# 137 GpSimd operations of an attention-and-FFN kernel each get a wait on the VectorE operation planned just ahead of them

## The chip, the cores and the metric

The kernel runs on one core of a Trainium2 chip. The metric is the device time of one execution in microseconds (us), from the runtime's own measurement; a run's time is a little longer than the span that the hardware profiler sees between the first and the last instruction. Names in the profile: PE is TensorE's matmul, PEld its weight load, DVE is VectorE, ACT is ScalarE, POOL is GpSimd, SP is SyncE, which only issues DMAs here.

## The reference, cut to what matters

Two stages follow each other. The first is causal attention with a choice of key chunks: for every query only the 6 chunks of 32 keys with the largest upper bound take part. The second is a gated feed-forward layer on the result.

```python
# q, k, v: (4, 8, 768, 64) float32
ub = np.sum(np.maximum(q*k_min, q*k_max), axis=-1)        # per query and chunk of 32 keys
top_chunks = np.argsort(np.where(causal, ub, -1e9))[..., -6:]
scores = q @ k.T / 8, kept where chunk is chosen and key <= query
attn = exp(scores - max) / sum;   x = (attn @ v) as (3072, 512)
gate = sigmoid(x @ w_gate);       out = (gate * (x @ w_val)) @ w_out      # d_ff 1536
```

## The kernel before, in words

**Tiling.** The 3072 tokens are cut into eight units, u0 to u7, of up to 384 tokens (three blocks of 128). For a unit the kernel chooses chunks (`choose`, lines 868 to 915: bounds on PE into `ub`, then on VectorE `ubn` transposes, `mx` finds the eight largest, `ap` compares with the sixth, `apt` transposes back, and `hqm` copies the result into the masked rows of `hqe`/`hqo`), attends (`attend`, lines 918 to 978: `sc` scores on PE, `exp` on ScalarE, `cm` the causal mask on GpSimd at line 952, `pv` on PE; then `rz` and `x` on VectorE, lines 987 and 989), and runs the feed-forward layer (`ffn`: `g` and `v` products on PE, `tanh` on ScalarE, `hg` on VectorE at line 1258, `o` on PE). Units 5 to 7 form part of the gate product, and units 4 to 7 the output product, from seven block products instead of eight. These need sums of blocks: `tw` (line 1031) and `ss` (1136) of weights, `sw`/`sx` (1047) of activations, `tt` (1149) of x. Units overlap in time: while one is in its feed-forward layer the next attends.

**What sets the order.** Every operation is recorded with `plan.add` under a name such as `cm_u4_6` (causal mask, unit 4, head 6), with the engines that may run it and the buffers it reads and writes. Nothing is decided at run time: the string `ORDER` names all operations in the order in which they are emitted, each with its engine (P, A, V, G, S for PE, ScalarE, VectorE, GpSimd, SyncE), and `SLOTS` gives each buffer its place. Both strings are the outcome of an earlier planning. Each engine runs its own operations strictly in that order. Between engines only semaphores order the work; they come from the data: an instruction waits for the writers of what it reads and for the readers of what it overwrites. An engine that has nothing to wait for starts its next operation at once, whatever time the plan had for it.

**GpSimd's work** is one list of 256 operations: masks (`cm`, `cmf`), casts of v into `v16` (line 651), copies and casts through the helper at line 434 (`hk`, `hq`, `hqm`, `k16`, `kn`, `qn`, `held`), sums (`tw`, `ss`, `sw`, `tt`, lines 1031, 1047, 1136, 1149), and, early on, the issue of the ten DMAs that load the feed-forward weights (`wg`, `wv`, `wo`). Many of these copies and sums can be on VectorE as well, and the plan has put some there. In `plan.add`, `port=True` marks operations for the planning as users of what GpSimd and VectorE have in common on the way to SBUF. It has no effect on what is emitted.

The loop that emits all this is the last statement of the kernel's function:

```python
    for op in plan.order():
        op.emit(op.engine)
```

Of the kernel before, what the change touches and what calls it, by code (L numbers as in the profile page):

```python
# [115 lines left out]
hk1_u1_0=G v16_0_2=G wo2=G mx1_u1=V ap1_u1=V apt1_u1=V hqm1_u1_0=V g_u0_5=P tanh_u0_5=A v_u0_5=P exp_u1_1_1=A hqm1_u1_2=A g_u0_6=P  # L116
# [7 lines left out]
kn_u2_0=G kT_u2_0=P kt_u2_0=A v_u0_11=P rz_u1_2=V xT_u1_0=V x_u1_2=V xps_u1_2=P q3_u2=S qn_u2_3=G qT_u2_3=P cm_u1_7=G pv_u1_7=P  # L124
# [5 lines left out]
hk1_u2_1=G hk0_u2_0=V hk0_u2_3=G kt_u2_2=A g_u1_1=P tanh_u1_1=A hk0_u2_2=A g_u1_0=P tanh_u1_0=A o0_u0_2=P expf_3_1=A cmf_3_0=G  # L130
# [3 lines left out]
hqm0_u2_2=G hq0_u2_3=G v16_0_4=G exp_u2_5_0=A cm_u2_5=G exp_u2_5_1=A exp_u2_0_0=A cm_u2_0=G v16_0_5=G hq1_u2_2=G hqm1_u2_2=G  # L134
# [18 lines left out]
x_u3_2=V qf0_u4_1=V sc_u3_1_1=P g_u2_2=P hqm1_u3_2=G sc_u3_6_2=P exp_u3_2_1=A sc_u3_0_1=P exp_u3_6_2=A tanh_u2_2=A sc_u3_6_0=P  # L153
exp_u3_6_0=A sc_u3_6_1=P exp_u3_6_1=A exp_u3_0_1=A g_u2_1=P tanh_u2_1=A sc_u3_1_2=P exp_u3_1_2=A sc_u3_1_0=P exp_u3_1_0=A
exp_u3_1_1=A hk0_1_3=G cm_u3_2=G pv_u3_2=P k01_2=S k11_2=S k10_2=S k00_2=S v_2_0=S k16_2_2=G kx1_2_1=V kx1_2_3=V kx0_2_1=V
k16_2_0=V out_u1_1=S o0_u1_2=P sc_u3_3_0=P exp_u3_3_0=A cm_u3_0=G pv_u3_0=P sc_u3_3_1=P exp_u3_3_1=A o1_u1_2=P sc_u3_3_2=P
# [17 lines left out]
qf0_u6_2=V hk0_2_3=G cm_u4_2=G v16_2_3=G k16_3_2=G k16_3_1=G osb_u2_1=V out_u2_1=S k16_3_0=V kt_3_2=V qm_u5_2=G sc_u4_0_1=P  # L174
# [5 lines left out]
hg_u3_7=V pv_u4_3=P sc_u5_0_0=P v_3_1=S q10_3=S q11_3=S q00_3=S q01_3=S xT_u4_0=S sc_u4_6_3=P exp_u4_6_3=A sc_u4_5_2=P  # L180
exp_u4_5_2=A sc_u4_6_2=P sc_u4_6_0=P exp_u4_6_0=A exp_u4_6_2=A sc_u4_6_1=P exp_u4_6_1=A cm_u4_4=G pv_u4_4=P cm_u4_5=G pv_u4_5=P
hq0_u5_2=G v16_2_2=G g_u3_10=P tanh_u3_10=A mx1_u5=V rz_u4_1=V ap1_u5=V x_u4_1=V kx0_3_2=V rz_u4_2=V apt1_u5=V x_u4_2=V kx1_3_2=V
xT_u4_2=S exp_u5_0_0=A sc_u5_1_0=P exp_u5_1_0=A sc_u5_1_2=P sc_u5_1_1=P sc_u5_0_2=P v16_2_4=G hqm0_u5_2=G g_u3_8=P tanh_u3_8=A
cm_u4_6=G pv_u4_6=P rz_u4_3=V hk0_3_1=G cm_u5_0=G exp_u5_1_2=A exp_u5_1_1=A v_u3_8=P hg_u3_8=V x_u4_3=V kt_3_0=V cm_u5_1=G
k16_3_3=G hqm1_u5_0=G v_3_3=S v_3_4=S xT_u4_1=S out_u2_2=S qf1_u6_2=V exp_u5_0_2=A sc_u5_2_0=P exp_u5_2_0=A sc_u5_2_2=P
sc_u5_3_1=P exp_u5_3_1=A sc_u5_3_2=P exp_u5_3_2=A sc_u5_3_0=P exp_u5_3_0=A pv_u5_1=P pv_u5_0=P v_u3_10=P hg_u3_10=V rz_u5_0=V
qf1_u6_3=V kt_3_3=V hq1_u5_2=G v16_3_0=G hqm1_u5_2=G sc_u5_4_1=P exp_u5_2_2=A exp_u5_4_1=A sc_u5_2_1=P sc_u5_5_0=P exp_u5_5_0=A
# [14 lines left out]
hg_u4_2=V tw0_1=G sc_u5_7_2=P hq1_u7_2=G exp_u5_7_0=A exp_u5_7_1=A exp_u5_7_2=A pv_u6_4=P pv_u6_5=P rz_u6_2=V x_u6_2=V apt1_u7=V  # L202
# [10 lines left out]
sw0_u4_1=V pv_u6_7=P sw1_u4_1=V rz_u6_3=V rz_u5_3=V sc_u7_4_0=P exp_u7_4_0=A xT_u6_1=S xT_u6_2=S sc_u7_4_3=P sc_u7_1_3=P  # L213
exp_u7_1_3=A sc_u7_4_1=P sc_u7_1_0=P exp_u7_1_0=A cm_u7_1=G exp_u7_4_3=A sc_u7_1_1=P exp_u7_4_1=A exp_u7_1_1=A p1_u4=P p1z_u4=P
p1s_u4=V ss1_g4=G sw1_u4_2=G sw3_u4_2=G sc_u7_1_2=P exp_u7_1_2=A x_u5_3=V pv_u7_2=P pv_u7_7=P x_u6_3=V tw2_2=V sc_u7_5_2=P
exp_u7_5_2=A p2_u4=P sc_u7_6_2=P exp_u7_6_2=A sc_u7_5_1=P sc_u7_6_0=P exp_u7_6_0=A exp_u7_5_1=A p2z_u4=P p6_u4=P p6z_u4=P c11_u4=V
sw3_u4_1=G sc_u7_6_3=P exp_u7_6_3=A sc_u7_5_3=P exp_u7_5_3=A sc_u7_5_0=P pv_u7_1=P sc_u7_6_1=P exp_u7_6_1=A sc_u7_4_2=P p5_u4=P
# [7 lines left out]
c3_g2_u5=V c12_g2_u5=V p7_g4_u5=P p4_g4_u5=P pv_u7_3=P rz_u7_1=V p1_g3_u5=P m1_g3_u5=A ss3_g4=G p5_g4_u5=P p3_g4_u5=P held_u4_5=G  # L225
c22_g2_u5=V x_u7_1=V c21_g2_u5=V tt0_u6=G p2_g3_u5=P p6_g3_u5=P p7_g3_u5=P p4_g3_u5=P cm_u7_5=G ss3_g3=G pv_u7_5=P pv_u7_4=P
# [22 lines left out]
hg_u6_7=V held_u6_2=G sw2_u6_0=G sw2_u6_2=G sw1_u6_0=G sw2_u6_1=G v_u6_6=P p1s_u6=A tanh_u6_6=A tanh_u7_3=A hg_u6_6=V sw0_u6_1=G  # L249
# [11 lines left out]
u4_u7=V p7_u7=P p7z_u7=P c12_u7=V c22_u7=V c21_u7=V out_u7_1=S out_u7_0=S held_u6_5=A p2z_u67=P p6_u67=P p6z_u67=P p5_u67=P  # L261
# [89 lines left out]
p1_u7:5 p26_u7:6 p5_u7:2 p3_u7:7 p7_u7:1 p4_u7:3 p1_u67:7 p26_u67:0 p5_u67:4 p3_u67:5 p7_u67:6 p4_u67:2  # L351
"""


def act(n, psum=True, parts=128):
    took = (170 if psum else 195) + n / 1.2
    return (took - 105 if parts == 128 else took + 10, took)
# [22 lines left out]
def kernel(  # L380
# [10 lines left out]
    nc = tc.nc  # L391
# [44 lines left out]
    def lone(name, shape, dtype=F16):  # L436
        return keep.tile(shape, dtype, tag=name, name=name)

    ident32 = lone("ident32", [128, 128], F32)
    ident16 = lone("ident16", [128, 128])  # L440
# [12 lines left out]
    def const(name, engines, emit, reads=(), writes=(), prio=-2.0, port=False):  # L453
        plan.add(name, engines, emit, reads, writes, prio, port=port)
# [93 lines left out]
    for i in range(2):  # L548
        const(f"kcr{i}", {DVE: (270, 280)}, lambda e, i=i: nc.vector.memset(kcr[i], 0.0),
              writes=[("kcr", i, jb, p, m) for jb in range(NBLK) for p in range(NP) for m in range(2)], prio=-8 if i == 0 else -1)  # L550
    for e_ in range(2):
        const(f"hq{e_}", {DVE: (150, 160)}, lambda e, e_=e_: nc.vector.memset(hq[1][e_][MASK[e_], :, 0:64], 0.0),
              writes=[("hqm", 1, e_, p, "zero") for p in range(NP)])
    for i in range(2):
        const(f"ap{i}", {DVE: (400, 410)}, lambda e, i=i: nc.vector.memset(ap[i], 0.0),
              writes=[("ap", i, 0), ("ap", i, 1)], prio=-0.5 + i)
        const(f"v1{i}", {POOL: (260, 300)}, lambda e, i=i: nc.gpsimd.memset(v16[i][:, :, :, D:D + 1], 1.0),
              writes=[("v16", i, jb) for jb in range(NBLK)], prio=-9 + 6 * i)
        for e_ in range(2):
            for o in range(2):  # L560
# [3 lines left out]
                      reads=[epat], writes=[("hkp", i, e_, p) for p in range(o, NP, 2)], prio=0.3 + 0.2 * i, port=True)  # L564
# [8 lines left out]
    for i in range(30):  # L573
        keep_awake(i)
    const("ident16", {DVE: (150, 230)}, lambda e: nc.vector.tensor_copy(ident16, ident32),
          reads=["ident32"], writes=["ident16"], prio=-1.0)


    wgs = moe_w_gate.rearrange("(c p) f -> p c f", p=128)
# [535 lines left out]
    for n, w in enumerate(combos):  # L1115
        if n < 6:
            b = Buf("v", f"ss_{w[0]}{w[1]}", [128, 4, 2, 128], F16)
# [272 lines left out]
    attend(units[7], 7.0)  # L1390
    ffn(units[7], 8.0, 0.95)

    for op in plan.order():
        op.emit(op.engine)


# [28 lines left out]
```

## Time and profile before

| | us |
|---|---|
| three runs, median (lowest to highest) | 282.64 (281.72 to 282.82) |
| the profiled execution | 283.43 |
| its span in the profile | 281.7 |
| VectorE busy, share of the span | 235.7, 84% |
| ScalarE busy | 180.5, 64% |
| GpSimd busy | 163.3, 58% |

The profiled execution is 1.7 us longer than its span, and 0.8 us longer than the median of the three runs. Its TensorE clock was granted in full (9 in all 40 slices of the page). "Busy" is the time in which an engine had an instruction in work; in the timeline a row gives an instruction's start, its length, and in brackets the time that its engine sat idle before it with what ended the wait. Rows of equal instructions that follow each other are merged (x3).

### The profile page before, as it was taken

How to read it: one execution, taken by the hardware profiler on the slowest of the kernel's cores; microseconds unless marked ns; L12 is line 12 of the kernel's file. 1: busy time of each engine (PE TensorE's matmuls, PEld its weight loads, DVE VectorE, ACT ScalarE, POOL GpSimd, SP SyncE). 2: the span in 40 equal slices, each digit the busy share in tenths (PEclk: the TensorE clock that was granted, in tenths of full speed). 3: DMA queues.
4: the chain of work that ended last, by engine and by line, in shares of the span. 5: the costliest groups of instructions: out<-in, count | busy, mean ns of one | idle time of the engine just before them, and what ended most of it. 6: DMA issues, size and time to landing. Idle time of an engine off the chain costs nothing.

```text
span 281.7 us, 7507 instructions
## 1 busy us (share of the span) xinstructions
PE 268.8 (95%) x2806; PEld 188.9 (67%) x2806; DVE 235.7 (84%) x686; ACT 180.5 (64%) x386; POOL 163.3 (58%) x262
## 2 busy tenths in 40 slices
PE   5868989999999999999999999999999999999994
PEld 4645657667855665556687657776888688778683
DVE  4889846697998998886999987977889998888885
ACT  6377868669957943559689979987983422341520
POOL 5797743638464781823869956842685568063450
PEclk9999999999999999999999999999999999999999
DMA  6999999899999598977897230100310033000304
GB/s 161 246 254 204 205 216 209 180 192 210 178 214 182 131 195 162 199 142 141 164 154 111 63 89 16 40 0 2 73 74 2 1 81 126 2 1 2 150 2 150
DMA packets 131717, 34.70 MB, mean 123 GB/s; under 512 B 119776, under 2 KB 128736, under 8 KB 131680
## 3 DMA queue, kind: packets, MB, share of 16 engines
q1 hardware_dynamic: 126912, 29.50, 50.2%
q0 software_dynamic: 4768, 4.72, 10.0%
q8 instruction: 22, 0.36, 0.6%
q14 instruction: 15, 0.12, 0.1%
HBM read 30.67 MB, written 6.29 MB: 131 GB/s over the span
## 4 chain that ended last, share of the span: by engine, by line
PE 81%; DMA 9%; DVE 6%; issue 1%; SPq 1%; POOL 0%; DVEq 0%; POOLq 0%
PE v_u L1237 19%; PE g_u L1237 14%; PE o_u L1286 11%; PE sc_u L935 11%; PE p_u L1060 10%; PE pv_u L968 6%; DMA wg<-in_moe_w_gate_dram 6%; PE p_g_u L1169 5%; PE ube_u L874 3%; DMA kq_u<-in_k_dram 2%; DMA kf<-in_k_dram 1%; DVE x_u L989 1%; DVE tw L1031 1%; DVE ox L1077 1%; DVE hg_u L1258 1%
## 5 line engine op out<-in xcount | busy, mean ns | idle before, releaser
L946 ACT ACTIVATE att_u<-sc_u 128x512 f16<-128x512 f32 (+3 forms) x184 | 86.8, 571 | 8.6 <-PE sc_u L935 7.3
L1237 PE MATMUL v_u<-xT_u,wv 128*128 128x384 f16 x384 | 72.4, 326 | 0.1
L1258 DVE SCALAR_TENSOR_TENSOR hg_u<-gate_u,v_u 128x384 f16<-128x384 f16 x96 | 51.0, 544 | 18.6 <-ACT gate_u L1249 9.3
L1249 ACT ACTIVATE gate_u<-g_u 128x384 f16<-128x384 f32 x72 | 35.2, 498 | 42.2 <-PE g_u L1237 36.9
L1237 PE MATMUL g_u<-xT_u,wg 128*128 128x384 f16 x288 | 56.0, 326 | 2.1 <-DMA wg<-in_moe_w_gate_dram 1.5
L952 POOL TENSOR_SCALAR_AFFINE_SELECT att_u<-att_u 128x384 f16<-128x384 f16 (+1 forms) x56 | 28.5, 517 | 40.9 <-ACT att_u L946 39.8
L1237 PEld LDWEIGHTS <-wv 128*128 128x128 f16 x384 | 36.1, 98 | 20.5 <-DMA wv<-in_moe_w_val_dram 0.4
L1237 PEld LDWEIGHTS <-wg 128*128 128x128 f16 x288 | 26.7, 98 | 19.5 <-DMA wg<-in_moe_w_gate_dram 3.0
L1286 PE MATMUL o_u<-wo,hg_u 128*128 128x512 f16 x144 | 34.3, 379 | 0.0
L968 PE MATMUL pv_u<-v,att_u 128*128 128x65 f16 x640 | 26.3, 193 | 0.0
L968 PEld LDWEIGHTS <-att_u 128*128 128x128 f16 x640 | 24.2, 98 | 2.9 <-issue 0.6
L1206 DVE TENSOR_TENSOR f_g_u<-p_g_u,f_g_u 128x192 f32<-128x192 f32 (+1 forms) x72 | 24.9, 384 | 1.0 <-PE p_g_u L1169 0.4
L935 PE MATMUL sc_u<-hqe,hke 128*128 128x128 f16 (+2 forms) x220 | 25.4, 243 | 0.2
L935 PE MATMUL sc_u<-hqo,hko 128*128 128x128 f16 (+2 forms) x220 | 24.1, 243 | 0.1
L1286 PEld LDWEIGHTS <-hg_u 128*128 128x128 f16 x144 | 13.7, 98 | 13.4
L935 PEld LDWEIGHTS <-hke 128*128 128x128 f16 x220 | 16.5, 98 | 5.3 <-issue 0.8
L935 PEld LDWEIGHTS <-hko 128*128 128x128 f16 x220 | 16.4, 98 | 4.7 <-issue 0.4
L651 POOL CAST v<-v 128x512 f16<-128x512 f32 x23 | 14.5, 633 | 3.0 <-DMA v<-in_v_dram 2.5
L1249 ACT ACTIVATE gate_u<-f_g_u 128x384 f16<-128x384 f32 x24 | 11.9, 519 | 5.6 <-DVE hg_u L1258 2.9
L989 DVE TENSOR_TENSOR x_u<-pv_u,rz_u 128x384 f16<-128x384 f32 (+1 forms) x28 | 14.6, 524 | 0.9 <-DMA xT_u<-x_u 0.5
L897 DVE MAX8 mx_u<-ubn_u 128x8 f32<-128x8 f32 (+16 forms) x152 | 12.7, 159 | 0.3
L841 DVE STREAM_TRANSPOSE qf_u<-q 128x384 f32<-128x384 f32 (+2 forms) x28 | 11.7, 437 | 1.2 <-DMA q<-in_q_dram 1.2
(187 smaller groups left out, 507.9 us busy)
## 6 DMA issues: line engine op xcount, KB each, us to landing
v<-in_v_dram SPq DMA_DIRECT2D x23, 256.0 KB, 4.7
k<-in_k_dram SPq DMA_DIRECT2D x12, 384.0 KB, 5.5
q<-in_q_dram SPq DMA_DIRECT2D x12, 384.0 KB, 5.5
out_dram<-osb_u SPq DMA_DIRECT2D x12, 256.0 KB, 3.4
out_dram<-sw SPq DMA_DIRECT2D x8, 256.0 KB, 2.1
wv<-in_moe_w_val_dram POOLq DMA_DIRECT2D x3, 512.0 KB, 10.2
wo<-in_moe_w_out_dram POOLq DMA_DIRECT2D x3, 512.0 KB, 18.9
qf<-in_q_dram SPq DMA_DIRECT2D x8, 128.0 KB, 3.4
```

Of the source, the lines that this page charges most:

```text
L651: plan.add(f"v16_{b}_{ib}", {POOL: pool(H * D)}, lambda e: nc.gpsimd.tensor_copy(v16[b % 2][:, ib, :, 0:D], at(t)), reads=[t], writes=[("v ...
L935: nc.tensor.matmul(at(t)[:, o:o + 128 * m], hk[b % 2][e_][:, p, 128 * jb:128 * jb + 128], hq[u.side][e_][:, p, 128 * x:128 * (x + m)], sta ...
L946: plan.add(f"exp_{u.name}_{h}_{y}", {ACT: act(n)}, lambda e, t=t, att=att, b0=b0, n=n: nc.scalar.activation(at(att)[:, b0:b0 + n], at(t), ...
L952: nc.gpsimd.affine_select(out=dv, in_=dv, compare_op=ALU.is_ge, fill=0.0, base=0, pattern=[[0, u.m], [1, 128]], channel_multiplier=-1)
L968: nc.tensor.matmul(at(pv)[:, last, x, :], at(att)[:, c:c + 128], v16[b % 2][:, jb, h, :], start=(jb == 0), stop=(jb == ib))
L989: plan.add(f"x_{u.name}_{p}", {DVE: dve(u.t)}, lambda e: nc.vector.tensor_tensor(at(x_).rearrange("p a (e d) -> p e a d", e=2), at(pv)[:, ...
L1060: nc.tensor.matmul(at(to)[:, side], a(j)[:, i], b(j)[:, i], start=j == i == 0, stop=j == 2 and i == 1)
L1206: plan.add(f"{p}_{name}", {POOL: pool2(192 * n), DVE: dve(192 * n)} if slow else {DVE: dve(192 * n)}, lambda e: both(e).tensor_tensor(dst( ...
L1237: nc.tensor.matmul(at(t), w16[:, c, 128 * fb:128 * fb + 128], at(u.xt)[:, c, :], start=(c == 0), stop=(c == 3))
L1249: plan.add(f"tanh_{u.name}_{fb}", {ACT: act(T, not seven[0])}, lambda e, gv=gv, gate=gate: nc.scalar.activation(at(gate), gv(), AF.Tanh, s ...
L1258: plan.add(f"hg_{u.name}_{fb}", {DVE: dve(T)}, lambda e, vv=vv, gate=gate, hg=hg, fb=fb: nc.vector.scalar_tensor_tensor(at(hg)[:, fb % 2], ...
L1286: nc.tensor.matmul(at(o), at(hgs[fc // 2])[:, fc % 2, 128 * tb:128 * tb + 128], wo16[:, fc, lo:hi], start=(fc == 0), stop=(fc == NFB - 1))
```

## The change

A string `TIES` lists 137 pairs `a<b`: `a` is an operation of GpSimd and `b` the operation of VectorE that the plan has ending last before `a` starts. As each `a` is emitted, it is given a dependency on the last instruction of `b`, with a semaphore, as if `a` read what `b` wrote. Nothing else of the program moves: the order on every engine, the engines, the buffers and the data are the same. In the built program GpSimd waits for VectorE's semaphore in 163 places instead of 47; its instructions that do nothing but wait are 120 instead of 60, since a wait beyond an instruction's own goes into one of these ahead of it. ScalarE and TensorE lose one such wait each, which the new ones imply. `ident16` is marked `port=True`, which emits nothing.

```diff
+TIES = """
+hqm0_u1_2<hqm0_u1_0 v16_0_3<hg_u0_1 hk1_u1_0<ubm1_u1 v16_0_2<hg_u0_2 v16_0_1<hqm1_u1_0 cm_u1_1<hk1_u1_3 qn_u2_2<kcr1
...
+hq0_u4_2<qm_u4_2 hq0_u4_0<qf0_u6_1 hq1_u4_0<qf0_u6_3 kcr_2<hg_u2_11 hk0_2_2<mx1_u4 cm_u4_1<qf0_u5_2 cm_u4_2<hg_u3_0
+k16_3_2<qf0_u6_2 qm_u5_2<k16_3_0 cm_u4_7<kt_3_1 cm_u4_3<hqm0_u5_0 cm_u4_5<rz_u4_0 hq0_u5_2<hg_u3_6 v16_2_2<hg_u3_7 v16_2_4<rz_u4_1
+hqm0_u5_2<x_u4_1 cm_u4_6<kx0_3_2 hk0_3_1<rz_u4_2 cm_u5_0<x_u4_2 k16_3_3<rz_u4_3 hqm1_u5_0<x_u4_3 v16_3_0<qf1_u6_2
+hqm1_u5_2<rz_u5_0 cm_u5_3<qf1_u6_3 hk1_3_1<kt_3_3 hq0_u7_2<hk0_3_3 cm_u5_5<qf0_u7_1 v16_3_2<x_u5_1 hq0_u7_0<ubn1_u6
+hqm1_u6_2<hqm1_u6_0 v16_2_5<rz_u5_2 cm_u6_3<x_u5_2 cm_u6_2<ubn1_u7 cm_u6_4<mx1_u7 hqm0_u6_0<rz_u6_1 cm_u6_5<x_u6_1 tw0_1<hg_u4_0
+hq1_u7_2<hg_u4_2 cm_u6_0<tw0_0 cm_u6_1<ap0_u7 cm_u5_7<apt0_u7 v16_3_5<hqm0_u7_2 cm_u7_7<tw1_1 v16_3_3<ss0_g4 sw2_u4_0<tw2_1
+cm_u7_2<hg_u4_6 cm_u6_7<hg_u4_7 cm_u7_1<sw0_u4_1 ss1_g4<rz_u5_3 sw1_u4_2<p1s_u4 sw3_u4_1<x_u6_3 cm_u7_6<tw2_2 cm_u7_3<tw3_1
...
+sw2_u6_2<c4_g3_u7 sw1_u6_0<c12_g3_u7 sw2_u6_1<hg_u6_7 sw1_u67_0<sw0_u7_0 sw3_u7_0<hg_u7_4 sw1_u7_1<hg_u7_11 sw3_u7_2<sw1_u67_2
+sw3_u67_2<c11_u7 sw3_u67_1<u4_u7 sw2_u67_2<c12_u7
+"""
...
-          reads=["ident32"], writes=["ident16"], prio=-1.0)
+          reads=["ident32"], writes=["ident16"], prio=-1.0, port=True)
...
+    ties = {}
+    for w in TIES.split():
+        a, b = w.split("<")
+        ties.setdefault(a, []).append(b)
+    ends = {}
+    traced = nc.cur_bb.bb.instructions
     for op in plan.order():
+        n = len(traced)
         op.emit(op.engine)
+        for b in ties.get(op.name, ()):
+            tc.add_manual_dep(traced[n], ends[b], mybir.DependencyInfo(mybir.DependencyClass.Sync, mybir.DependencyReason.DATA), reason="tie")
+        ends[op.name] = traced[-1].name
```

More of the change, by code (lines that the diff above doesn't have):

```diff
@@ L352 @@
 """
+TIES = """
+hqm0_u1_2<hqm0_u1_0 v16_0_3<hg_u0_1 hk1_u1_0<ubm1_u1 v16_0_2<hg_u0_2 v16_0_1<hqm1_u1_0 cm_u1_1<hk1_u1_3 qn_u2_2<kcr1
+cm_u1_5<rz_u1_0 cm_u1_4<x_u1_0 kn_u2_0<qf_u2_2 qn_u2_3<rz_u1_2 cm_u1_7<xT_u1_0 cm_u1_6<x_u1_2 qm_u2_1<hg_u0_11 hq1_u2_1<kx1_u2_0
+hq0_u2_1<rz_u1_3 vc_3<qm_u2_3 hk1_u2_1<kcr_u2 hk0_u2_3<hk0_u2_0 cmf_3_1<hqm1_u2_0 cm_u2_4<hqm0_u2_0 hqm0_u2_2<rzf_3_1
+hq0_u2_3<xf_3_1 cm_u2_1<hg_u1_2 k16_1_1<kx0_1_3 hk1_u2_2<rz_u2_0 cm_u2_3<hg_u1_1 cm_u2_2<rz_u2_2 cm_u2_6<rz_u2_1 cm_u2_7<x_u2_1
+k16_1_3<x_u2_3 cm_u3_5<hqm0_u3_0 cm_u3_4<qf0_u4_0 cm_u3_2<qf0_u4_3 k16_2_2<x_u3_2 cm_u3_0<qf0_u4_1 hk1_1_3<kx1_2_1 v16_1_5<kx1_2_3
+cm_u3_3<k16_2_0 cm_u3_7<kt_2_2 hk1_2_0<rz_u3_0 k16_2_3<kx0_2_0 v16_2_0<hg_u2_0 k16_2_1<rz_u3_3 hk0_2_0<x_u3_1 v16_2_1<qf1_u4_0
+hq0_u4_2<qm_u4_2 hq0_u4_0<qf0_u6_1 hq1_u4_0<qf0_u6_3 kcr_2<hg_u2_11 hk0_2_2<mx1_u4 cm_u4_1<qf0_u5_2 cm_u4_2<hg_u3_0
[5 more added lines that the diff above has]
+cm_u7_2<hg_u4_6 cm_u6_7<hg_u4_7 cm_u7_1<sw0_u4_1 ss1_g4<rz_u5_3 sw1_u4_2<p1s_u4 sw3_u4_1<x_u6_3 cm_u7_6<tw2_2 cm_u7_3<tw3_1
+ss2_g1<held_u4_3 ss3_g2<c22_u4 ss3_g4<c11_g1_u5 held_u4_5<c4_g1_u5 tt0_u6<c12_g1_u5 cm_u7_5<c21_g1_u5 ss3_g3<c11_g2_u5
+tt1_u6<c3_g2_u5 held_u4_0<c22_g2_u5 tt2_u6<c21_g2_u5 cm_u7_0<c11_g3_u5 sw0_u5_0<hg_u5_6 sw2_u45_0<c11_g2_u6 sw2_u5_0<sw2_u45_1
+sw0_u5_1<sw1_u5_0 sw1_u5_1<hg_u5_8 sw3_u5_2<c22_g4_u6 sw2_u5_2<c3_g2_u6 sw0_u45_1<c22_g2_u6 sw1_u45_1<c11_u5 sw0_u45_2<u4_u5
+sw1_u45_2<c12_u5 sw3_u45_1<c22_u5 sw3_u45_2<c21_u5 tt0_u7<c11_u45 tt3_u7<c22_g1_u6 held_u6_2<hg_u6_8 sw2_u6_0<c11_g3_u7
+sw2_u6_2<c4_g3_u7 sw1_u6_0<c12_g3_u7 sw2_u6_1<hg_u6_7 sw1_u67_0<sw0_u7_0 sw3_u7_0<hg_u7_4 sw1_u7_1<hg_u7_11 sw3_u7_2<sw1_u67_2
+sw3_u67_2<c11_u7 sw3_u67_1<u4_u7 sw2_u67_2<c12_u7
+"""
 def act(n, psum=True, parts=128):
```

## The prediction

> **What bounds the kernel now.** I began with the page's first rows, for the share of each engine.
>
> ```profile
> span 281.7 us, 7507 instructions
> PE 268.8 (95%) x2806; PEld 188.9 (67%) x2806; DVE 235.7 (84%) x686; ACT 180.5 (64%) x386; POOL 163.3 (58%) x262
> ```
>
> TensorE has work for 268.8 of 281.7 us, GpSimd for 163.3. A wait added to GpSimd therefore costs only where TensorE comes to feel it, and a gain can only come out of TensorE's remaining 12.9 us. Where those lie is in the busy time by stretch: start and end of the stretch, its length, then busy us and instructions of PE, PEld, DVE, ACT and POOL, the clock, and the DMA columns.
>
> ```profile
> 20.00:42.60 22.60, 20.39 (x186) 12.86 (x187) 16.42 (x58) 17.05 (x43) 14.78 (x27) 1.00 1.21 209
> 42.60:60.00 17.40, 17.40 (x199) 11.89 (x200) 12.30 (x38) 11.98 (x31) 7.77 (x17) 1.00 1.05 198
> 60.00:140.00 80.00, 80.00 (x809) 51.05 (x808) 69.63 (x193) 56.15 (x123) 46.31 (x71) 1.00 0.92 174
> 140.00:160.00 20.00, 20.00 (x273) 15.01 (x271) 18.69 (x60) 18.54 (x38) 15.88 (x25) 1.00 0.71 118
> 160.00:180.00 20.00, 19.93 (x296) 13.00 (x294) 17.25 (x82) 17.60 (x34) 14.03 (x21) 1.00 0.23 56
> 180.00:200.00 20.00, 19.77 (x214) 13.87 (x214) 16.61 (x44) 17.15 (x37) 8.16 (x15) 1.00 0.06 11
> 200.00:240.00 40.00, 40.00 (x434) 33.22 (x432) 36.16 (x94) 19.19 (x43) 27.38 (x41) 1.00 0.20 58
> ```
>
> From 42.6 to 240 us TensorE lacks 0.07 + 0.23 = 0.30 us, all between 160 and 200. Before 42.6 it waits for data and weights, and the first pair of the change starts at 29.3 us. So the kernel is bound by TensorE's own work, and I looked for the places where it still waits for VectorE. In TensorE's weight loads, which show a wait more sharply than the matmuls with their modelled ends, three waits stand in that region (the brackets give the idle time).
>
> ```profile
> 179.93 0.43 PEld L935 LDWEIGHTS <-hke 128*128 128x128 f16 x6 [0.19 <-issue]
> 180.63 0.22 PEld L935 LDWEIGHTS <-hke 128*128 128x128 f16 x3 [0.27 <-DVE x_u L989]
> 190.54 0.20 PEld L935 LDWEIGHTS <-hko 128*128 128x128 f16 x2 [0.36 <-issue]
> ```
>
> Together they are 0.19 + 0.27 + 0.36 = 0.82 us. The chain of waits runs over VectorE just there: the pieces before the first two waits are these.
>
> ```profile
> 177.68 0.45 DVE hg_u L1258
> 178.13 0.18 DVE ap L902
> 178.32 0.87 issue
> ...
> 179.33 0.54 DVE hg_u L1258
> ```
>
> **The change part by part: what it can give.** The 0.87 us without a name lie inside one VectorE operation. Here is the timeline around it (start, length, engine).
>
> ```profile
> 177.60 0.54 DVE L1258 SCALAR_TENSOR_TENSOR hg_u<-gate_u,v_u 128x384 f16<-128x384 f16 x1
> 177.94 1.15 POOL L1031 TENSOR_TENSOR tw<-wo 128x512 f16<-128x512 f16 x1
> 178.05 1.36 DVE L902 TENSOR_TENSOR ap<-ubn_u,mx_u 128x288 f16<-128x288 f32 x1
> 180.01 0.56 DVE L989 TENSOR_TENSOR x_u<-pv_u,rz_u 128x384 f16<-128x384 f32 x1
> 181.69 0.74 DVE L1031 TENSOR_TENSOR tw<-wo 128x512 f16<-128x512 f16 x1
> 182.35 0.76 DVE L902 TENSOR_TENSOR ap<-ubn_u,mx_u 128x288 f16<-128x288 f32 x1
> ```
>
> The same `ap` form takes 0.46 us where GpSimd is idle, and `tw` on VectorE 0.42:
>
> ```profile
> 122.50 0.46 DVE L902 TENSOR_TENSOR ap<-ubn_u,mx_u 128x288 f16<-128x288 f32 x1
> 190.93 0.42 DVE L1031 TENSOR_TENSOR tw<-wo 128x512 f16<-128x512 f16 x1
> ```
>
> At 178.05 `ap1_u7` started 0.11 us after GpSimd's `tw0_1`, and ended at 179.41, 0.32 after that had ended at 179.09: it stood still until GpSimd was through. Its excess is 1.36 - 0.46 = 0.90 us; at 181.69 and 182.35 the excesses are 0.32 and 0.30.
>
> Now the pair `tw0_1<hg_u4_0`. `hg_u4_0` is the operation at 177.60, over at 178.14. GpSimd's `tw0_1` can then start no earlier than about 178.2, when `ap1_u7`, which follows `hg_u4_0` directly, has been running since 178.05. So `ap1_u7` takes 0.46, and GpSimd stands back instead. The `hg` at 179.33 comes earlier, and the wait at 179.93, which ended when that `hg` did (179.87), goes. `rz` and `x_u` behind it then wait for `pv` alone, which TensorE reaches 0.19 earlier too; so the 0.27 go as well. What is late next is TensorE's own list.
>
> The third wait, at 190.54, ends with an `x_u` for which VectorE had come from 186.83 without a break, beginning with this pair of rows:
>
> ```profile
> 186.73 0.67 POOL L1047 TENSOR_TENSOR sw<-hg_u 128x256 f16<-128x256 f16 x1
> 186.83 0.85 DVE L1031 TENSOR_TENSOR tw<-wo 128x512 f16<-128x512 f16 x1
> ```
>
> Excess 0.85 - 0.42 = 0.43. By the pair `sw2_u4_0<tw2_1` GpSimd's sum waits until past 191.35 (the `tw` at 190.93, 0.42 long); the 0.43 cover the 0.36. The gain is at most 0.82 us, at least zero if held GpSimd work collides elsewhere on that path. I take 0.82, since each collision has its own pair that undoes it.
>
> The Trainium skill, "SBUF — State Buffer", section "Who interferes with whom", says that a VectorE operation with at most one input in SBUF and outside the 2-port modes does not contend with GpSimd. By that rule 108 of the 137 named VectorE operations (`rz`, `x`, `hg`, the `c` sums and others that read PSUM or reduce) have nothing that a wait could protect, and only the operation behind them may have. That speaks against most of the pairs, and against a gain beyond the collisions; the `ap` and `tw` rows, with two SBUF inputs each, agree with it.
>
> **What it can cost.** I set each pair against the timeline: start of the GpSimd operation, end of the VectorE operation. In 57 pairs the VectorE operation is over already, and the wait is met. In 80 it is not, and GpSimd would be held. The first and the last of the 80:
>
> ```profile
> 29.30 0.32 DVE L432 COPY hqe<-apt_u 64x640 f16<-64x640 f16 x1
> ...
> 273.89 1.74 DVE L1077 SCALAR_TENSOR_TENSOR sw<-p_u,sw 128x256 f32<-128x256 f32 x3
> ```
>
> ```profile
> 29.34 0.87 POOL L434 COPY hqe<-apt_u 64x640 f16<-64x640 f16 x1 [0.85 <-DVE apt_u L908]
> ...
> 273.78 0.71 POOL L1047 TENSOR_TENSOR sx<-held,hg_u 128x256 f16<-128x256 f16 x1
> ```
>
> The longest hold is the copy `hk0_2_2` at 118.22, which must wait for the end of `mx1_u4` at 122.47: 4.25 us, in an idle time of 4.60 us that GpSimd has behind it anyway.
>
> ```profile
> 118.22 0.82 POOL L434 COPY hke<-kt 64x768 f16<-64x768 f16 x1
> 123.64 0.82 POOL L434 COPY hqo<-apt_u 64x768 f16<-64x768 f16 x1 [4.60 <-DVE apt_u L908]
> ```
>
> Behind a held instruction GpSimd's whole list waits, early on the issue of the last two weight DMAs too (29.62 + 0.06 - 29.34 = 0.34 us later, by the rows of the first pair). So I followed each hold down the list to its reader. The place with the least to spare is the busiest, 140 to 160 us (15.88 of 20 busy): `hqm1_u5_0<x_u4_3`.
>
> ```profile
> 150.41 0.82 POOL L434 COPY hqo<-apt_u 64x768 f16<-64x768 f16 x1
> ```
>
> ```profile
> 150.73 0.55 DVE L989 TENSOR_TENSOR x_u<-pv_u,rz_u 128x384 f16<-128x384 f32 x1
> ```
>
> ```profile
> 152.48 0.38 PE L935 MATMUL sc_u<-hqo,hko 128*128 128x384 f16 x2
> ```
>
> `x_u4_3` ends at 151.28. A start after VectorE's signal shows about 0.06 to 0.13 us of lag, bounded by two rows: `qf_u` from 162.65 for 0.57, then GpSimd at 163.35.
>
> ```profile
> 162.65 0.57 DVE L841 STREAM_TRANSPOSE qf_u<-q 128x384 f32<-128x384 f32 x1
> ```
>
> ```profile
> 163.35 0.82 POOL L434 CAST hqe<-qf_u 64x768 f16<-64x768 f32 x1 [1.32 <-DVE qf_u L841]
> ```
>
> That is 163.35 - 163.22 = 0.13. The copy then runs from 151.41 to 152.23, and its reader starts at 152.48: 0.25 to spare. Every other reader has as much or more. The cost on TensorE is zero, bounded above by the second rival below. Met waits cost GpSimd between nothing and 0.13 us each, at most 57 x 0.13 = 7.4 us in all of its 281.7 - 163.3 = 118.4 idle ones; I take nothing.
>
> **Sum.** Profiled execution: 283.43 = span 281.7 + 1.7 around it; less 0.82 it is 282.6. The median of the runs shown lies 0.79 below the profiled one, so I set the forecast against the median: 282.64 - 0.82 = 281.8 us.
>
> **The rivals.**
>
> *Nothing comes of it: 282.6.* The held GpSimd work is moved onto VectorE's next operations; a new collision of 0.4 us between 178 and 190 gives back half, two give back all. For it: GpSimd's held sums between 186 and 192 then meet VectorE's dense run of `tw` and `ss`. Against it: the operation behind a named one starts first, as `ap1_u7` does at 178.05.
>
> *Slower: 284.0.* Between 144 and 154 us the pairs close a ring: mask on GpSimd, `pv` on TensorE, `rz` and `x` on VectorE, and now back to GpSimd's next operation. If the lag of 0.13 adds up over the 13 pairs in this stretch, GpSimd falls 1.7 us back, TensorE stands for that less 0.25, and 282.64 + 1.4 is 284.0. It decides from 0.25 us of lag on. Against it: VectorE's times there are set by its own list (18.69 of 20 busy), so that lags do not add.
>
> *More: 280.9.* The modelled matmul ends hide waits for VectorE, whose excess beside GpSimd shrinks everywhere and not just at 178 to 190; another 0.9 us. Against it: 40.00 of 40.00 and 80.00 of 80.00.
>
> That the change doesn't do what it says is ruled out by the built program: each of the 137 waits stands on the instruction named.
>
> **How the numbers follow.** Forecast 0.57, nothing 0.25, more 0.12, slower 0.06. The range 280.8 to 283.1 takes in the forecast, nothing with the runs' spread of half a us, and most of "more". A measurement here can tell about 0.5%, 1.4 us. Faster by over that: most of "more" and a little of the forecast's upper side, 0.15; slower by over that: 0.06; within it 0.79.
>
> **What would show it.** Right: `ap1_u7` at 0.46 us, the three weight loads without idle time, `ap` and `tw` on VectorE near 0.46 and 0.42 between 178 and 188, GpSimd's idle time put down to VectorE, and TensorE's list unbroken around 149 to 155. Wrong: idle weight loads with hqo, hko or att_u behind GpSimd, or new excesses on VectorE's `tw` and `ss` at 186 to 192 with the wait at 190.54 still there.

## The result, and the profile after

The changed kernel took 281.52 us, the median of 22 runs (280.67 to 287.37), the kernel before 282.63 in 22 runs beside them (281.59 to 283.65). The ratio is 0.9966, 95% interval 0.9952 to 0.9981: a gain of 0.34%, or 1.0 us, between 0.5 and 1.4: within the half per cent set in the prediction, though the interval leaves out 1. The forecast was 281.8. Two runs are in a slow state and in none of the ratios, though in the ranges and medians: the 287.37 here, and one of 467.71 of the kernel before beside the last four kernels below.

The profiled execution took 281.46 us. The page of the kernel after, first rows:

```profile
span 279.8 us, 7565 instructions
...
PE 269.8 (96%) x2806; PEld 190.0 (68%) x2806; DVE 232.1 (83%) x686; ACT 180.5 (65%) x386; POOL 163.3 (58%) x262
```

VectorE is busy 3.6 us less than before (235.7), for the same 686 instructions; GpSimd's busy time is the same. The busy time by stretch (same columns as before) shows TensorE without a gap where it had lacked 0.07 and 0.23 us:

```profile
140.00:160.00 20.00, 20.00 (x272) 14.87 (x270) 18.61 (x56) 18.60 (x39) 16.54 (x25) 1.00 0.62 109
160.00:180.00 20.00, 20.00 (x302) 13.39 (x301) 16.96 (x85) 17.63 (x34) 13.63 (x21) 1.00 0.21 51
180.00:200.00 20.00, 20.00 (x219) 14.44 (x218) 15.96 (x43) 17.85 (x39) 9.14 (x16) 1.00 0.08 17
```

The weight loads in whose places the three waits stood (everything there is now 0.9 to 1.7 us earlier) carry no idle time in brackets any more:

```profile
178.54 0.91 PEld L957 LDWEIGHTS <-hke 128*128 128x128 f16 x14
...
188.67 0.37 PEld L957 LDWEIGHTS <-hko 128*128 128x128 f16 x3
```

And VectorE's `ap1_u7`, `tw0_0`, `ap0_u7` and `tw0_2` (1.36, 0.74, 0.76 and 0.85 us before) all stand at their undisturbed length, in the timeline of VectorE:

```profile
177.14 0.45 DVE L924 TENSOR_TENSOR ap<-ubn_u,mx_u 128x288 f16<-128x288 f32 x1
...
180.17 0.42 DVE L1053 TENSOR_TENSOR tw<-wo 128x512 f16<-128x512 f16 x1
180.50 0.45 DVE L924 TENSOR_TENSOR ap<-ubn_u,mx_u 128x288 f16<-128x288 f32 x1
...
185.42 0.42 DVE L1053 TENSOR_TENSOR tw<-wo 128x512 f16<-128x512 f16 x1
```

In GpSimd's timeline the two operations that did the damage now wait, and say for whom:

```profile
177.31 1.30 POOL L1053 TENSOR_TENSOR tw<-wo 128x512 f16<-128x512 f16 x1 [0.25 <-DVE hg_u L1280]
...
189.85 0.67 POOL L1069 TENSOR_TENSOR sw<-hg_u 128x256 f16<-128x256 f16 x1 [0.90 <-DVE tw L1053]
```

`tw0_1` starts 0.17 us behind `ap1_u7` instead of 0.11 ahead of it. That is the whole edit at this place.

**A sharper ruler than the total.** A gain of one us is hard to see in runs that spread over two. But TensorE's list runs almost unbroken from 58 us on, so I measured two distances inside each profile. The *stretch* is the time from TensorE's weight load of `kf` near 58 us to the start of its last group of output products. The *tail* is the time from that start to the end of VectorE's last five output sums (`ox`); the span ends 2.6 to 2.7 us behind these in every profile. The rows, in the timeline before,

```profile
58.66 0.23 PEld L724 LDWEIGHTS <-kf 64*128 64x128 f16 x8 [0.41 <-DVE hke L432]
...
276.00 3.06 DVE L1077 SCALAR_TENSOR_TENSOR ox<-p_u,ox 128x512 f32<-128x512 f32 x5
...
277.15 0.82 PE L1060 MATMUL p_u<-tw,hg_u 128*128 128x256 f16 x6
```

and after:

```profile
57.75 0.23 PEld L746 LDWEIGHTS <-kf 64*128 64x128 f16 x8 [0.41 <-DVE hke L454]
...
274.04 3.06 DVE L1099 SCALAR_TENSOR_TENSOR ox<-p_u,ox 128x512 f32<-128x512 f32 x5
...
275.45 0.82 PE L1082 MATMUL p_u<-tw,hg_u 128*128 128x256 f16 x6
```

Stretch: 277.15 - 58.66 = 218.49 before, 275.45 - 57.75 = 217.70 after, 0.79 less; that is the forecast 0.82. Tail: 276.00 + 3.06 - 277.15 = 1.91 before, 274.04 + 3.06 - 275.45 = 1.65 after, 0.26 less; that no step of the prediction had. Its cause stands in VectorE's and GpSimd's timeline at the end, before:

```profile
272.52 1.30 POOL L1047 TENSOR_TENSOR sx<-held,sx 128x256 f16<-128x256 f16 x2 [0.29 <-DVE sx L1047]
...
273.43 0.54 DVE L1047 TENSOR_TENSOR sx<-held,sx 128x256 f16<-128x256 f16 x1
```

and after:

```profile
271.73 0.28 DVE L1069 TENSOR_TENSOR sx<-held,sx 128x256 f16<-128x256 f16 x1
...
271.96 1.30 POOL L1069 TENSOR_TENSOR sx<-held,sx 128x256 f16<-128x256 f16 x2 [0.90 <-DVE sw L1099]
```

VectorE's sum fell from 0.54 to 0.28 us because GpSimd's sums of the same row now come behind it (pair `sw3_u67_2<c11_u7`), and at the end VectorE's list, not TensorE's, sets the time. Together 1.05 us. The spans differ by 1.9; the other 0.9 lie ahead of 58 us, and the experiments show that they need no pair.

### The profile page after: what moved, and what is told of

Its sections match the earlier page's. It is cut to its first block, busy times and chain, and to the rows that moved or that the text cites. A ratio compares the mean times of both kernels' runs of the same rounds, so it can differ in the third digit from the quotient of the medians.

```text
span 279.8 us, 7565 instructions
## 1 busy us (share of the span) xinstructions
PE 269.8 (96%) x2806; PEld 190.0 (68%) x2806; DVE 232.1 (83%) x686; ACT 180.5 (65%) x386; POOL 163.3 (58%) x262
## 4 chain that ended last, share of the span: by engine, by line
PE 84%; DVE 7%; DMA 6%; issue 1%; SPq 1%; POOL 0%; DVEq 0%
PE v_u L1259 20%; PE g_u L1259 15%; PE sc_u L957 12%; PE o_u L1308 11%; PE p_u L1082 8%; PE pv_u L990 7%; DMA wg<-in_moe_w_gate_dram 5%; PE p_g_u L1191 5%; PE ube_u L896 3%; DMA kf<-in_k_dram 1%; DVE ox L1099 1%; DVE xf L768 1%; DVE sw L1099 1%; DVE kcr L681 1%; DVE kx_u L681 1%
## 5 line engine op out<-in xcount | busy, mean ns | idle before, releaser
L1099 DVE SCALAR_TENSOR_TENSOR sw<-p_u,sw 128x256 f32<-128x256 f32 (+1 forms) x20 | 10.6, 529 | 3.0 <-PE p_u L1082 1.8
```

Source lines behind the costliest of these rows:

```text
L1099: plan.add(f"{p}_{name}", {DVE: dve(256 * n)}, lambda e: nc.vector.scalar_tensor_tensor(four()[:, lo], at(src) if n == 1 else at(src)[:, 0 ...
```

## The experiments

The numbers of all kernels first. Stretch and tail are read from the three rows shown above, in each kernel's own profile; the ratio is to the kernel before in the same session.

| kernel | pairs | median us | ratio, 95% interval | weight load of `kf` at | stretch | tail |
|---|---|---|---|---|---|---|
| before | 0 | | 1 | 58.66 | 218.49 | 1.91 |
| after | 137 | 281.52 | 0.9966 (0.9952 to 0.9981) | 57.75 | 217.70 | 1.65 |
| two | 2 | 281.50 | 0.9965 (0.9943 to 0.9986) | 57.20 | 217.70 | 1.91 |
| without four | 133 | 281.89 | 0.9994 (0.9964 to 1.0024) | 57.72 | 218.48 | 1.66 |
| early | 19 | 282.04 | 0.9994 (0.9974 to 1.0014) | 56.76 | 218.49 | 1.90 |
| middle | 56 | 282.11 | 0.9990 (0.9973 to 1.0008) | 56.94 | 218.50 | 1.91 |
| unshared | 108 | 281.29 | 0.9957 (0.9935 to 0.9980) | 56.90 | 218.01 | 1.65 |
| shared | 29 | 282.57 | 1.0015 (0.9989 to 1.0041) | 59.78 | 218.20 | 2.11 |
| ring | 3 | 282.35 | 1.0008 (0.9985 to 1.0031) | 57.07 | 218.49 | 1.92 |
| gate | 2 | 281.36 | 0.9976 (0.9951 to 1.0000) | 58.68 | 217.70 | 1.91 |
| tail | 1 | 281.74 | 0.9989 (0.9968 to 1.0011) | 57.25 | 218.49 | 1.65 |
| three | 3 | 281.26 | 0.9975 (0.9960 to 0.9989) | 56.95 | 217.70 | 1.65 |
| moved | 2 | 281.27 | 0.9979 (0.9965 to 0.9993) | 57.07 | 217.70 | 1.72 |
| behind | 1 | 281.59 | 0.9991 (0.9974 to 1.0008) | 57.35 | 217.99 | 1.90 |

The sessions' medians of the kernel before were 282.63 (for the kernel after), 282.33 (two to middle), 282.23 (unshared to gate) and 282.11 (tail to behind). What to see: the stretch takes 218.48 to 218.50, 218.20, 218.0 or 217.70 and nothing between, whatever the position of the `kf` weight load. Because these distances repeat, tenths of a us can be read from one profile each.

**Two pairs alone.**

```diff
 TIES = """
-(137 pairs)
+tw0_1<hg_u4_0 sw2_u4_0<tw2_1
 """
```

> Only two pairs are kept, tw0_1<hg_u4_0 and sw2_u4_0<tw2_1. Theory A (three collisions of GpSimd sums with VectorE's ap and tw hold TensorE up at 179.9, 180.6 and 190.5 us): the three idle times of TensorE's weight loads, 0.82 us in all before, are gone, ap1_u7 takes 0.46 us, tw0_2 0.42, and the time falls by 0.8 us (0.3%). Rival B (the early pairs let the gate weights land sooner, so that TensorE waits 0.8 instead of 1.7 us at 42 us): no change of the time, wait at 42 us as before. Rival C (all VectorE operations relieved a little): under 0.1 us.

Stretch 217.70, as with all 137; ratio 0.9965. Two pairs do all that the change does on TensorE's list. The tail stays at 1.91: these two have no part in it.

**All but four.**

```diff
-tw0_1<hg_u4_0 ... cm_u7_7<tw1_1 v16_3_3<ss0_g4 sw2_u4_0<tw2_1
+(the other 133 pairs as they were)
```

> All pairs but four: tw0_1<hg_u4_0, cm_u7_7<tw1_1, v16_3_3<ss0_g4 and sw2_u4_0<tw2_1 are left out, so that GpSimd's sums at 178 and 186.7 us start as before. Theory A: the three waits of TensorE are back (about 0.2, 0.3 and 0.3 us), time within 0.3 us of the kernel before, 0.8 above the changed one. Rival B: the wait at 42 us is short (0.8), time 0.9 us under before. Rival C: nearly the whole gain stays, about 1 us under before.

The three waits are back with their old lengths, in TensorE's weight loads of this kernel:

```profile
178.99 0.43 PEld L955 LDWEIGHTS <-hke 128*128 128x128 f16 x6 [0.18 <-issue]
179.68 0.22 PEld L955 LDWEIGHTS <-hke 128*128 128x128 f16 x3 [0.27 <-DVE x_u L1009]
...
189.59 0.20 PEld L955 LDWEIGHTS <-hko 128*128 128x128 f16 x2 [0.36 <-issue]
```

Stretch 218.48, as before, with 133 waits on GpSimd: they give nothing on TensorE's list and cost nothing there. The tail is 1.66: its pair is among the 133.

**The first 19 pairs, and the 56 between 61 and 170 us.**

```diff
+hqm0_u1_2<hqm0_u1_0 v16_0_3<hg_u0_1 ... hk0_u2_3<hk0_u2_0        (early: 19)
+cmf_3_1<hqm1_u2_0 cm_u2_4<hqm0_u2_0 ... hq0_u7_0<ubn1_u6         (middle: 56)
```

> Only the 19 pairs up to 58 us. Theory A: time as before within 0.2 us, the three late waits there. Rival B: TensorE's wait for the gate weights at 42 us 0.8 us instead of 1.7, time 0.9 us lower. Rival C: 0.2 us lower.

> Only the 56 pairs from 61 to 170 us, with the ring of mask, product and VectorE's rz and x at 144 to 154. Theory A: time as before within 0.2 us; no idle time of TensorE's weight loads from 140 to 160 us that wasn't there before (0.25 us to spare at the copy hqm1_u5_0). Rival C: 0.5 us lower. Rival of the forecast (lags of 0.13 us add up round the ring): 1.4 us slower, with new waits of TensorE from 149 us on.

Neither changes stretch or tail. With the other profiles they settle a rival that the traces of before and after had raised: TensorE's wait for the gate weights near 42 us was 1.66 us before and 0.79 after. In weight loads of before, after and the kernel with two pairs:

```profile
42.56 1.09 PEld L1237 LDWEIGHTS <-wg 128*128 128x128 f16 x8 [1.66 <-DMA wg<-in_moe_w_gate_dram]
```

```profile
41.80 1.09 PEld L1259 LDWEIGHTS <-wg 128*128 128x128 f16 x8 [0.79 <-DMA wg<-in_moe_w_gate_dram]
```

```profile
41.25 1.09 PEld L1241 LDWEIGHTS <-wg 128*128 128x128 f16 x8 [0.62 <-DMA wg<-in_moe_w_gate_dram]
```

The last of them has no pair ahead of 176 us, so up to here it is the kernel before, instruction for instruction, and it waits 0.62. The 1.66 was that execution's: the `kf` weight load comes at 58.66 there, and at 56.94 to 57.35 in seven other profiles whose programs have no pair ahead of it either (two, middle, ring, tail, three, moved, behind). So the 0.9 us of the spans' difference that lie ahead of 58 us are within the scatter of executions without any early pair, most of it the wait for this load. Whether the early pairs are worth a few tenths either way, a ratio of 0.9994 (0.9974 to 1.0014) can't tell.

**By what the named operation uses.**

```diff
+v16_0_3<hg_u0_1 hk1_u1_0<ubm1_u1 ... tw0_1<hg_u4_0 ... sw2_u67_2<c12_u7     (unshared: 108)
+hqm0_u1_2<hqm0_u1_0 v16_0_1<hqm1_u1_0 ... sw2_u4_0<tw2_1 ... sw3_u7_2<sw1_u67_2     (shared: 29)
```

> Only the 108 pairs whose named VectorE operation reads PSUM, reduces or transposes, so that by the Trainium skill, "SBUF — State Buffer", section "Who interferes with whom", it needs no protection from GpSimd itself. tw0_1<hg_u4_0 is one of them, sw2_u4_0<tw2_1 isn't. Theory A (what counts is the operation behind the named one): ap1_u7 takes 0.46 us, the waits near 178.5 and 179.2 us (0.19 and 0.27) are gone, the one near 189.6 (0.36) stays; 0.46 us less than before, a ratio of 0.998. Rival (a pair helps only the operation that it names): ap1_u7 stays at 1.36 us, all three waits stay, no gain.

> Only the other 29 pairs, whose named VectorE operation takes two inputs from SBUF or copies within it; sw2_u4_0<tw2_1 is one of them, tw0_1<hg_u4_0 isn't. Theory A: ap1_u7 stays at 1.36 us and the first two waits stay (0.19 and 0.27), the third (0.36) goes; 0.36 us less than before, a ratio of 0.9987. Rival (a pair helps only the operation that it names): these 29 bring the whole gain, 0.82 us, a ratio of 0.997.

With the 108 only the third wait is left, with the 29 only the first two:

```profile
188.28 0.20 PEld L953 LDWEIGHTS <-hko 128*128 128x128 f16 x2 [0.37 <-issue]
```

```profile
181.05 0.43 PEld L942 LDWEIGHTS <-hke 128*128 128x128 f16 x6 [0.19 <-issue]
181.75 0.22 PEld L942 LDWEIGHTS <-hke 128*128 128x128 f16 x3 [0.27 <-DVE x_u L996]
```

Stretches 218.01 and 218.20: 0.48 and 0.29 less than before, 0.77 in sum where both together give 0.79. So a pair isn't judged by the operation that it names, but by which operation GpSimd's then no longer meets. With `tw0_1<hg_u4_0` that is `ap1_u7`, behind the named `hg`, which needs no protection itself. With `sw2_u4_0<tw2_1` it is `tw0_2`, which stands eleven places ahead of the named one on VectorE's list. The medians go the same way but further apart than the stretches: by stretch and tail the kernel with 108 gains 0.48 + 0.26 = 0.74 us, the one with 29 gains 0.29 - 0.20 = 0.09, and the measured -1.2 and +0.4 us have intervals that hold these. The profile of the kernel with 29 is of the slowest of its twelve runs (284.44). In it a load of v landed late, which held GpSimd's list:

```profile
37.65 0.61 POOL L658 CAST v<-v 128x512 f16<-128x512 f32 x1 [3.74 <-DMA v<-in_v_dram]
```

TensorE's weight load of `att_u` stands 1.89 us for a mask behind this cast, and the `kf` weight load comes at 59.78. Whether one of its early pairs has a part in that is open; the kernel with 19 early pairs, which has the pair of this cast too, shows nothing of it (56.76). Its tail is longer than before's, 2.11. In VectorE's timeline at the end two sums stand that were 0.73 and 0.54 us before:

```profile
272.48 0.29 DVE L1054 TENSOR_TENSOR sx<-sx,held 128x256 f16<-128x256 f16 x1
...
274.26 0.73 DVE L1054 TENSOR_TENSOR sx<-held,sx 128x256 f16<-128x256 f16 x1
```

The pair `sw3_u7_2<sw1_u67_2` freed the first of them, GpSimd's sums came later by that, and the second met the next one from its start. A wait here moved a collision to where it costs.

**One wait too many, in the ring.** The prediction gave the copy `hqm1_u5_0` 0.25 us to spare. This kernel holds it for one VectorE operation more.

```diff
+tw0_1<hg_u4_0 sw2_u4_0<tw2_1 hqm1_u5_0<kt_3_0
```

> The two pairs of theory A and hqm1_u5_0<kt_3_0, which holds the GpSimd copy at 150.4 us (after's time) for one VectorE operation more, until about 151.3, 0.85 us later. By the working of the prediction that copy has 0.25 us to spare before TensorE's scores: theory (little spare): TensorE stands near 151.5 us for about 0.6 us, and the time is 0.2 us below before instead of 0.8, a ratio near 0.9993. Rival (the ring has more room than that, TensorE's scores of another part or the queue ahead of them take it up): no wait there and a ratio of 0.997, as with the two pairs alone.

GpSimd's copy after, by its own pair, and in this kernel:

```profile
150.44 0.82 POOL L456 COPY hqo<-apt_u 64x768 f16<-64x768 f16 x1 [0.16 <-DVE x_u L1011]
```

```profile
150.64 0.82 POOL L438 COPY hqo<-apt_u 64x768 f16<-64x768 f16 x1 [1.76 <-DVE kt L829]
```

```profile
151.51 0.10 PEld L939 LDWEIGHTS <-hko 128*128 128x128 f16 x1 [0.69 <-issue]
```

Counted from the `kf` weight load the copy starts at 150.64 - 57.07 = 93.57 instead of 150.44 - 57.75 = 92.69: 0.88 later. TensorE's weight load stands for 0.69 us of it, and the whole stretch is 0.79 longer than with the two pairs. So the ring bites, and a hold of 0.88 gives back the whole gain, 0.2 more than expected. The spare behind the pair's own hold is then 0.1 to 0.2 us (0.88 less 0.79 or 0.69), a little under the 0.25 worked out.

**The gate weights' load, earlier.**

```diff
-kt_u1_1=V hk0_u1_1=G wg2=G qm_u1_2=A
+kt_u1_1=V wg2=G hk0_u1_1=G qm_u1_2=A
 (and the two pairs)
```

> The two pairs of theory A, and the last load of the gate weights is issued on GpSimd's queue ahead of the copy hk0_u1_1 instead of behind it: the copy stood idle for 1.6 us there, waiting for VectorE, so the load leaves about 2 us earlier. TensorE's wait for these weights near 41 us was 0.57 to 0.93 us in the profiles of the changed kernels. If the issue sets the landing: that wait goes and TensorE starts 0.6 us earlier, a ratio near 0.995. Rival (the transfers share their engines, so an earlier issue lands no earlier, or the load takes from the loads ahead of it): the wait stays, a ratio of 0.997.

The wait stayed (0.72 us) and so did the time. But the load did not leave earlier in this profile. Here is its issue in GpSimd's timeline, in the kernel with two pairs and in this one:

```profile
25.95 0.74 POOL L594 DMA_DIRECT2D wg<-in_moe_w_gate_dram  x1
```

```profile
26.60 0.75 POOL L594 DMA_DIRECT2D wg<-in_moe_w_gate_dram  x1
```

It now follows the issue ahead of it (a load of `wv`, 25.86 instead of 23.14) directly, but the list had come there 2.72 us later, in part by a wait of 1.24 us that the other kernel didn't have. So whether an earlier issue lands earlier stays open. The `kf` weight load came at 58.68, inside the scatter of 1.7 us at this place, and a gain of 0.6 can't be seen there in one profile.

**The tail's pair alone, and the three together.**

```diff
+sw3_u67_2<c11_u7                                        (tail)
+tw0_1<hg_u4_0 sw2_u4_0<tw2_1 sw3_u67_2<c11_u7           (three)
```

> One pair alone, sw3_u67_2<c11_u7, of the last stage, which no step of the prediction priced. In the profiles of the kernels that have it, VectorE's sum sx<-held,sx ahead of the last output sums takes 0.28 us instead of 0.54, and VectorE's last output sum starts 0.69 us after TensorE's last matmul instead of 0.94. Theory (a fourth collision, on VectorE's list at the end): 0.25 us less from TensorE's last matmul to the end of the span, nothing else; a ratio near 0.9991. Rival (the tail is set by the stores or by another late pair): the tail stays at 4.0 us.

> Three pairs: tw0_1<hg_u4_0, sw2_u4_0<tw2_1 and sw3_u67_2<c11_u7. Theory (four waits, three pairs, and nothing in the other 134): 0.79 us less from 58 us to TensorE's last matmul and 0.25 us less behind it, as the kernel with all 137; a ratio of 0.9963, which the kernel with all of them can't beat. Rival (the other pairs have a share too): less than all 137, near 0.998.

The first of these texts counts its tail, 4.0 us, from the start of TensorE's last single matmul to the end of the span; the table counts to the end of VectorE's last sum. Alone, the pair leaves the stretch at 218.49 and takes the tail to 1.65. With the other two, the timeline gives the same three distances as the kernel with 137 pairs:

```profile
56.95 0.23 PEld L728 LDWEIGHTS <-kf 64*128 64x128 f16 x8 [0.41 <-DVE hke L436]
...
273.24 3.06 DVE L1081 SCALAR_TENSOR_TENSOR ox<-p_u,ox 128x512 f32<-128x512 f32 x5
...
274.65 0.82 PE L1064 MATMUL p_u<-tw,hg_u 128*128 128x256 f16 x6
```

274.65 - 56.95 = 217.70, 273.24 + 3.06 - 274.65 = 1.65. On its page VectorE is busy for 233.8 us:

```profile
PE 269.2 (96%) x2806; PEld 190.1 (68%) x2806; DVE 233.8 (84%) x686; ACT 180.4 (65%) x386; POOL 162.9 (58%) x262
```

That is 1.9 less than before, where all 137 pairs take 3.6. Part of both lies ahead of 58 us, where VectorE's busy time scatters from 40.5 to 42.1 us among kernels without a pair there. So here is the busy time from the `kf` weight load to the end of the span (columns as in the prediction), before, with three pairs and with all:

```profile
58.66:281.70 223.04, 219.01 (x2336) 155.47 (x2328) 193.67 (x565) 141.21 (x301) 126.07 (x192) 1.00 0.49 100
```

```profile
56.95:279.00 222.05, 218.51 (x2336) 155.38 (x2328) 192.11 (x565) 141.11 (x301) 125.73 (x192) 1.00 0.49 101
```

```profile
57.75:279.80 222.05, 218.52 (x2336) 155.43 (x2328) 190.99 (x565) 141.17 (x301) 126.51 (x193) 1.00 0.49 101
```

All 137 pairs take 193.67 - 190.99 = 2.68 us off VectorE's 565 instructions there, three take 1.56, and the time is the same 222.05: the other collisions that the 134 avoid lay beside TensorE's work. Even `ap0_u7`, at 0.45 us with all pairs, takes 0.77 here and nothing waits for it:

```profile
179.92 0.77 DVE L906 TENSOR_TENSOR ap<-ubn_u,mx_u 128x288 f16<-128x288 f32 x1
```

The interval of the ratio holds both the expected 0.9963 and the rival's 0.998, so it can't decide between them; the distances do.

**The sum moved instead of the wait.**

```diff
-c11_u7=V sw3_u67_0=V
+c11_u7=V sw3_u67_0=G
 (and the first two pairs)
```

> The first two pairs, and in the last stage no pair, but the sum sw3_u67_0 is given to GpSimd, ahead of its other three of that row, instead of VectorE. VectorE's list at the end then lacks that sum's 0.20 us of start to start as well as its collision. Theory (VectorE's list sets the end): the last output sum starts 0.45 us earlier than in the kernel before, 0.2 us earlier than with the pair; 1.25 us less in all, a ratio of 0.9956, which beats both kernels. Rival (GpSimd's four sums in a row come too late for the first output sum, or TensorE's products set the end by then): no better than the pair, 0.9963.

The tail is 1.72, not the 1.46 expected, and not better than with the pair. GpSimd now starts its sums earlier, and another VectorE sum pays, in the timeline of this kernel:

```profile
269.80 2.02 POOL L1051 TENSOR_TENSOR sx<-held,sx 128x256 f16<-128x256 f16 x3
...
269.92 0.75 DVE L1051 TENSOR_TENSOR sw<-hg_u 128x256 f16<-128x256 f16 x1
```

0.75 us instead of 0.28: it starts 0.12 behind GpSimd's. VectorE's output sums behind it then start later:

```profile
270.59 2.92 DVE L1081 SCALAR_TENSOR_TENSOR sw<-p_u,sw 128x512 f32<-128x512 f32 x5
```

That is 274.77 - 270.59 = 4.18 us ahead of TensorE's last group, where it is 274.90 - 270.57 = 4.33 in the kernel with two pairs. So of the 0.45 us expected 0.19 came, 0.15 went to the new collision, and where the other 0.11 went no row shows. No kernel here beats the changed one by a measurable amount.

**Behind the operation itself.**

```diff
+tw0_1<ap1_u7
```

> One pair, tw0_1<ap1_u7: GpSimd's weight sum waits for the end of the operation that it collided with, instead of the end of the one ahead of it. Theory (the two share something, and whoever starts second pays): ap1_u7 at 0.46 us, tw0_1 at 1.15 us instead of the 1.30 that it takes behind hg_u4_0, the waits of 0.19 and 0.27 gone, the one of 0.36 still there; 0.48 us less, a ratio of 0.9983. Rival (1.30 us is what the later start costs in itself, by what else runs then): tw0_1 stays at 1.30.

```profile
176.74 0.45 DVE L906 TENSOR_TENSOR ap<-ubn_u,mx_u 128x288 f16<-128x288 f32 x1
...
177.28 1.16 POOL L1035 TENSOR_TENSOR tw<-wo 128x512 f16<-128x512 f16 x1 [0.61 <-DVE ap L906]
```

The first two waits are gone here too (stretch 217.99, 0.50 less), and `tw0_1` takes 1.16 us instead of the 1.30 that it takes just behind `hg_u4_0`. The 0.14 are what GpSimd pays there when it comes second.

## Why the prediction was right, and what it missed

- **The three waits, 0.82 us: right.** The stretch is 0.79 shorter. Each collision had its pair as said: `tw0_1<hg_u4_0` frees the first two waits (0.48 alone), `sw2_u4_0<tw2_1` is among the 29 that free the third alone (0.29, where its row had 0.36).
- **Nothing on TensorE's list from the other 135 pairs: right.** Two pairs give the stretch of all 137, and without the four pairs around the waits it is what it was.
- **"The gain is at most 0.82 us": wrong, by the tail's 0.26.** The failing step is the search: it looked for TensorE's waits from 42.6 to 240 us and took TensorE's list for the end of the program. Behind its last matmul VectorE's list sets the time, and there GpSimd held up one sum by 0.26 us. The rows stood in the trace of before: the sum took 0.54 beside a GpSimd sum, and 0.28 just ahead. With 0.82 + 0.26 the forecast would have been 281.6. That the total fits 281.8 too is no merit of it: the measured gain is known only to between 0.5 and 1.4 us, and 0.26 is lost in that.
- **Held GpSimd work costs nothing: right, with a little less to spare than said.** After, the copy at 150.44 us waits 0.16 and TensorE's stretch shows nothing; held 0.88 us longer it costs 0.79, so that 0.1 to 0.2 us were to spare and not 0.25. That no other reader has less, the prediction only said; the stretch of 217.70 with all pairs shows that none ran short. The rival *slower* did not come: with the 56 pairs of the middle, the ring's 13 among them, the stretch is 218.50, so the lags don't add up to anything that TensorE sees.
- **The rival *nothing*** expected new collisions among `tw` and `ss` at 186 to 192 us. One came, a `tw` of 0.67 instead of 0.42, in VectorE's timeline after, and no wait of TensorE follows it:

```profile
188.56 0.67 DVE L1053 TENSOR_TENSOR tw<-wo,tw 128x512 f16<-128x512 f16 x1
```

- **The rival *more*** (every excess of VectorE hides a cost) is out: 2.68 us less of VectorE's busy time from 58 us on give no more than 1.56 do.
- **The Trainium skill, "SBUF — State Buffer", section "Who interferes with whom"**: that `hg`, `rz` or `x` need no wait for their own sake agrees with what is seen (`hg` takes 0.55 us either way). As a filter for the pairs it would have thrown out two of the three that count: `hg_u4_0` and `c11_u7` read PSUM, and the operations behind them are what those pairs protect. The same section says that issue order decides who blocks; the trace agrees: 0.11 us of head start for GpSimd cost VectorE 0.90, 0.17 for VectorE cost GpSimd 0.14.

## What to carry to other kernels

Instructions that grow beside another engine cost only what the list that sets the end waits for them: of the 2.68 us that VectorE was relieved of from 58 us on, 1.05 counted, and three waits in the right places give all of that. Search the whole span, the end too, for the engine that sets the time there; behind TensorE's last matmul it was another one. And where runs scatter by a us or two from the loads at the start, measure a distance inside the profile, from a row past the scatter to the last one: here it repeated to 0.02 us among kernels with the same waits.

## What the runs showed of the hardware

- Whoever came second lost what was left of the first one's time, but for 0.13 to 0.14 us, on both engines. VectorE behind GpSimd: `ap1_u7` overlapped `tw0_1` by 1.04 us and took 0.90 longer; `tw0_2` overlapped `sw2_u4_0` by 0.57 and took 0.43 longer; after, the `tw` at 188.56 overlapped GpSimd's cast by 0.39 and took 0.25 longer. GpSimd behind VectorE: `tw0_1` overlapped `ap1_u7` by 0.28 and took 0.14 longer; before, a cast overlapped `ap0_u7` (182.35 to 183.11) by 0.35 and took 0.83 instead of 0.61. So 0.90 against 0.14 doesn't come from the engine, but from how much of the first one was still to come. Here are the two casts in GpSimd's timeline, after and before; five pairs of rows are not a rule, and no run shows what the 0.14 are.

```profile
188.34 0.61 POOL L673 CAST v<-v 128x512 f16<-128x512 f32 x1
```

```profile
182.76 0.83 POOL L651 CAST v<-v 128x512 f16<-128x512 f32 x1
```

- VectorE's 128x256 f16 sum takes 0.28 us alone and 0.72 to 0.75 when it starts 0.09 to 0.12 us behind a GpSimd sum of the same shape, whose 0.67 don't change.
- The point at 58 us scatters by 1.7 us between executions of the same instructions (56.94 to 58.66), about the spread of the runs' times. TensorE's wait for the landing of a gate weight load, 0.21 to 1.66 us in the same profiles, is a part of it.
